# The cosine's argument in turns: one VectorE operation for two in a fused DeltaNet and cosine-gated layer

## The chip, the cores and the metric

The kernel runs on one NeuronCore of a Trainium2 chip. The metric is the device time of one execution in microseconds (us), from the first to the last instruction, as the median of several executions. The core has a matrix engine (TensorE, PE in the profile, with its weight loads listed apart as PEld), a vector engine (VectorE, DVE), an activation engine (ScalarE, ACT), a general engine (GpSimd, POOL) and a queue engine that here only starts transfers (SyncE, SP). Every engine runs its own list of instructions in order and waits on semaphores for the others.

## The reference

Two blocks follow each other. The first is a delta-rule recurrence over 768 steps for 4 batches and 8 heads of width 48. The second multiplies the resulting 3072 x 384 matrix by `w_in` (384 x 2048), applies a gate h cos(h) to each element, and multiplies by `w_out` (2048 x 384).

```python
for t in range(S):
    kt, vt, bt = (k_n[:, :, t], v[:, :, t], beta[:, :, t, None])
    y[:, :, t] = np.einsum('bhd,bhde->bhe', q[:, :, t], state)
    v_old = np.einsum('bhde,bhd->bhe', state, kt)
    state = state + bt[:, :, :, None] * np.einsum('bhd,bhe->bhde', kt, vt - v_old)
...
h = x @ w_in
g = h * np.cos(h)
return (g @ w_out).astype(np.float32)
```

The change lies in the cosine of the second block.

## The kernel before

The recurrence is cut into 24 units of 32 steps. For a pair of units a triangular system is inverted, on VectorE for the first pair and on GpSimd for the other eleven, and carried through DRAM into the shape that the next matmuls want. Each unit then runs through the matmuls `turn`, `gram`, `state`, `solve`, `update`, `within` and `features` on TensorE. A pair of units gives 256 tokens, and these go through the second block as pair p: 8 steps of `hidden`, then the products with `w_out`. For all pairs but the first, those products use Strassen's scheme: seven half-size products for eight, with sums of the gates formed on VectorE (`left_sum`, L829) and the results gathered there (`collect`, L861).

The weights arrive as 64-bit numbers in 28 tiles and are cut down to float32 on the core: a transfer (`narrow_load`), two ScalarE operations (`narrow_split`), two VectorE operations (`narrow_shift`, L414 and L419) and one GpSimd operation (`narrow_add`, L423). The weights are scaled by 256 on the way, so that the first layer's result in PSUM is 256 h (`SCALE = 256.0`).

One step of the first layer computes 2 x 128 hidden features for 256 tokens. It fills a PSUM tile `p_h`, of which there are two; a tile comes free only when the gate has read it. This is the part that the change touches:

```python
def hidden_turns(p, f):                                # ScalarE, L735
    turns[p, f] = ffn_pool.tile([128, 2, TOK], I32, name="turns")
    nc.scalar.activation(
        turns[p, f], p_hs[p, f], AF.Copy, scale=1.0 / (2.0 * math.pi * SCALE)
    )

def hidden_rest(p, f):                                 # VectorE, L742 and L745
    r = rests[p, f] = ffn_pool.tile([128, 2, TOK], FP, name="r")
    n = turns.pop((p, f))
    nc.vector.scalar_tensor_tensor(
        out=r, in0=n, scalar=-PI2_HI * SCALE, in1=p_hs[p, f], op0=ALU.mult, op1=ALU.add
    )
    nc.vector.scalar_tensor_tensor(
        out=r, in0=n, scalar=-PI2_LO * SCALE, in1=r, op0=ALU.mult, op1=ALU.add
    )

def hidden_cos(p, f):                                  # ScalarE, L751 and L752
    r = rests[p, f]
    nc.scalar.activation(r, r, AF.Abs)
    nc.scalar.activation(r, r, AF.Sin, bias=halfpi, scale=-1.0 / SCALE)

def hidden_gate(p, f):                                 # VectorE, L759
    ...
    nc.vector.tensor_tensor(
        out=gates[p, f // 4][:, f % 4 : f % 4 + 2],
        in0=rests.pop((p, f)), in1=p_hs.pop((p, f)), op=ALU.mult,
    )
```

The first operation writes the number of whole turns in h as an integer. The two VectorE operations subtract that many times 2 pi, in two parts of 2 pi so as to keep precision; what is left is an angle between -pi and pi (times 256). The cosine is then the sine of pi/2 minus its absolute value.

The order of the instructions on each engine is fixed when the kernel is written out, by a list scheduler inside the kernel (`class Order`). It knows for each task an engine, a cost in us, what it depends on, and a due time; due times run backward from the `hidden` and output tasks. At each moment an engine takes, of the tasks that may run, the one that is due first, with two rules that matter here: no task may run whose due time is more than `WINDOW` beyond the most urgent one's, and TensorE prefers to stay with small matmuls or with large ones as long as the next of the same sort is due at most `STICK` later:

```python
WINDOW = 82.51
STICK = 2.55
SMALL = ("gram", "state", "solve", "update", "within")
...
W_IN, W_OUT, LOADS = 57.87, 95.11, -8.12      # when weight tiles are due, and their loads
START = 35.79                                 # when the first hidden step is due
FIRST, STEP = 3.55, 5.99                      # pace of the hidden steps, first pair and later ones
BASE = [START + (8 * FIRST + (p - 1) * 8 * STEP if p else 0) for p in range(NU // 2 + 2)]
...
add(("hidden", *key), "PE", 2.62, lambda f=f: hidden(p, f), deps,
    makes=[("h", ("h", *key))], uses=[("x", p)],
    due=BASE[p] + f // 2 * (STEP if p else FIRST))
add(("turns", *key), "ACT", 0.65, lambda f=f: hidden_turns(p, f), ...)
add(("rest", *key), "DVE", 1.45, lambda f=f: hidden_rest(p, f), ...)
add(("cos", *key), "ACT", 1.45, lambda f=f: hidden_cos(p, f), [("rest", *key)])
add(("gate", *key), "DVE", 0.73, lambda f=f: hidden_gate(p, f), ...)
```

The weight tiles arrive in a shared ring of 9 buffers (`GATES = 9`), which the gates use too; a tile holds its buffer until `narrow_add` has read it.

Of the kernel before, what the change touches and what calls it, by code (L numbers as in the profile page):

```python
# [14 lines left out]
ALU = mybir.AluOpType  # L15
AF = mybir.ActivationFunctionType
# [1 line left out]
C = 32  # L18
DP = 64
SPLIT = 2  # L20


PI2_HI = 6.28125
PI2_LO = 2.0 * math.pi - PI2_HI


SCALE = 256.0
# [23 lines left out]
class Order:  # L51
# [6 lines left out]

    WINDOW = 82.51
    LAG = {"PE": 0.2, "DVE": 0.15, "ACT": 0.15, "POOL": 0.2, "SP": 2.0}
    IN_FLIGHT = 8
    STICK = 2.55
    CHANGE = 0.15
    SMALL = ("gram", "state", "solve", "update", "within")

# [12 lines left out]
    def add(  # L80
        self, key, engine, cost, emit, deps=(), makes=(), uses=(), moves=0.0, due=1e9
    ):

        assert key not in self.tasks, key
        self.tasks[key] = [engine, cost, due, emit, set(deps), makes, uses, moves]
        for t in uses:
            self.users[t] = self.users.get(t, 0) + 1
        for tag, t in makes:
            self.tiles[t] = tag
# [19 lines left out]
    def run(self, wrote):  # L109
# [28 lines left out]
        while events:  # L138
# [21 lines left out]
            def fits(key):  # L160
                return all(live[tag] < self.bufs[tag] for tag, _ in self.tasks[key][5])

            dues = list(running.values())
            for heap in ready.values():
                dues.append(min((x[0] for x in heap if fits(x[2])), default=1e9))
            limit = min(dues) + self.WINDOW
            for engine, heap in ready.items():
# [6 lines left out]
                if engine == "PE":  # L174
                    if (item[2][0] in self.SMALL) != small:
                        item = min(
                            (
                                x for x in able
                                if x[0] <= item[0] + self.STICK
                                and (x[2][0] in self.SMALL) == small  # L180
# [43 lines left out]
def kernel(  # L224
# [32 lines left out]
    nc = tc.nc  # L257
# [90 lines left out]
    for b in range(B):  # L348
        nc.gpsimd.dma_start(
            out=bq[C * b : C * b + H].rearrange("p n t -> p (n t)"), in_=beta[b]  # L350
# [6 lines left out]
    halfpi = const.tile([128, 1], FP, name="halfpi")  # L357
# [359 lines left out]
    gates, p_hs, turns, rests, p_os, outs = ({} for _ in range(6))  # L717

    def hidden(p, f):
        p_h = p_hs[p, f] = bank("h", [128, 2, TOK], "p_h")  # L720
        for i in range(2):
            for t in range(KT):
                nc.tensor.matmul(  # L723
                    p_h[:, i],
                    w_in[:, t, (f + i) * 128 : (f + i + 1) * 128],
                    xts[p][:, t],
                    start=(t == 0),
                    stop=(t == KT - 1),
                )

    def hidden_turns(p, f):
        turns[p, f] = ffn_pool.tile([128, 2, TOK], I32, name="turns")
        nc.scalar.activation(  # L735
            turns[p, f], p_hs[p, f], AF.Copy, scale=1.0 / (2.0 * math.pi * SCALE)
        )

    def hidden_rest(p, f):
        r = rests[p, f] = ffn_pool.tile([128, 2, TOK], FP, name="r")  # L740
        n = turns.pop((p, f))
        nc.vector.scalar_tensor_tensor(  # L742
            out=r, in0=n, scalar=-PI2_HI * SCALE, in1=p_hs[p, f], op0=ALU.mult, op1=ALU.add
        )
        nc.vector.scalar_tensor_tensor(  # L745
            out=r, in0=n, scalar=-PI2_LO * SCALE, in1=r, op0=ALU.mult, op1=ALU.add
        )

    def hidden_cos(p, f):
        r = rests[p, f]  # L750
        nc.scalar.activation(r, r, AF.Abs)  # L751
        nc.scalar.activation(r, r, AF.Sin, bias=halfpi, scale=-1.0 / SCALE)  # L752

    def hidden_gate(p, f):
        if f % 4 == 0:
            gates[p, f // 4] = ffn_pool.tile(
                [128, 4, TOK], FP, name="g_ffn", tag="g", bufs=GATES
            )
        nc.vector.tensor_tensor(  # L759
            out=gates[p, f // 4][:, f % 4 : f % 4 + 2],  # L760
            in0=rests.pop((p, f)),
            in1=p_hs.pop((p, f)),
            op=ALU.mult,
        )
# [120 lines left out]
    )  # L885
    add = order.add
    VECTOR = {0: "one"}
    W_IN, W_OUT, LOADS = 57.87, 95.11, -8.12
    PLAIN = range(1)
    outs_done = [None]  # L890
    START = 35.79
    FIRST, STEP = 3.55, 5.99
    BASE = [START + (8 * FIRST + (p - 1) * 8 * STEP if p else 0) for p in range(NU // 2 + 2)]

    def inverse(m):
# [113 lines left out]
    def gated(p):  # L1009
        for f in range(0, FT, 2):  # L1010
            deps = [("features_out", 2 * p + 1)]
            if p == 0:
                deps += [("add", t) for t in range(KT * (f // 4 + 1))]
            if p or f:
                deps.append(("hidden", p if f else p - 1, f - 2 if f else FT - 2))
            key = (p, f)
            add(("hidden", *key), "PE", 2.62, lambda f=f: hidden(p, f), deps,
                makes=[("h", ("h", *key))], uses=[("x", p)],
                due=BASE[p] + f // 2 * (STEP if p else FIRST))
            add(("turns", *key), "ACT", 0.65, lambda f=f: hidden_turns(p, f),  # L1020
                [("hidden", *key)], makes=[("turns", ("turns", *key))])
            add(("rest", *key), "DVE", 1.45, lambda f=f: hidden_rest(p, f),
                [("turns", *key)], makes=[("r", ("r", *key))], uses=[("turns", *key)])
            add(("cos", *key), "ACT", 1.45, lambda f=f: hidden_cos(p, f), [("rest", *key)])
            add(("gate", *key), "DVE", 0.73, lambda f=f: hidden_gate(p, f),
                [("cos", *key)] + ([("gate", p, f - 2)] if f % 4 else []),
                makes=[] if f % 4 else [("g", ("gates", p, f // 4))],
                uses=[("h", *key), ("r", *key)], due=BASE[p] + f // 2 * STEP + 8)
        if p in PLAIN:
            plain(p)  # L1030
        else:
            strassen(p)
# [7 lines left out]
    def plain(p):  # L1040
        last = outs_done[0]
        for i in range(2):
            for k in range(FT // 4):
                deps = [("gate", p, 4 * k), ("gate", p, 4 * k + 2)]
                if p == 0:
                    deps += [("add", 12 + t) for t in range(4 * k + 4)]
                if last:
                    deps.append(last)
                last = ("out", p, i, k)
                add(last, "PE", 2.62, lambda i=i, k=k: output(p, i, k), deps,  # L1050
                    makes=[] if k else [("o", ("p_o", p, i)), ("o", ("p_o2", p, i))],
                    uses=[("gates", p, k)], due=BASE[p + 1] + (4 * i + k + 0.5) * STEP)
            add(("out_out", p, i), "ACT", 0.52, lambda i=i: output_out(p, i), [last],
                makes=[("o_out", ("o", p, i))], uses=[("p_o", p, i), ("p_o2", p, i)],
                due=BASE[p + 1] + (4 * i + 5) * STEP)
            store_task(p, i, [("out_out", p, i)], BASE[p + 1] + (4 * i + 6) * STEP)
        outs_done[0] = last
# [68 lines left out]
    for p in sorted(PLAIN):  # L1126
        gated(p)
    weight_sums()
    for p in range(len(PLAIN), NU // 2):
        gated(p)  # L1130
# [63 lines left out]
```

## Time and profile before

| | before |
|---|---|
| time, median of 3 executions | 717.2 us (714.33 to 720.22) |
| profiled execution | 712.6 us, mean granted TensorE clock 0.963 |
| hidden steps (12 pairs x 8) | 96 |
| first and last matmul of the first layer | 76.0 us, 679.9 us |
| ScalarE in the first layer (L735, L751, L752) | 57.0 + 60.5 + 69.3 us |
| VectorE for the Strassen sums (L829) | 81.6 us |
| GpSimd in the inversions (L580, L587) | 143.7 + 141.4 us |

The page of a profile gives busy time by engine, then the span in 40 slices of 17.8 us each with a digit for the busy tenths, then the chain of waits that ended last, then groups of instructions by source line. A group's row reads: line, engine, operation, what it writes `<-` what it reads, shape and type, how many times; then the total busy time and the mean duration in nanoseconds; then the idle time of the engine just before these instructions, and what ended most of it. Two further views are used: the waits (who waited for whom, in a chosen stretch of time) and a table of busy time by stretch, whose columns are length, then busy time and instruction count of PE, PEld, DVE, ACT and POOL, then the granted TensorE clock, the share of the transfer engines in use and the bytes moved.

### The profile page before, as it was taken

Reading aid. Unit: us, or ns where it says so; the run is one execution under the profiler, and the core shown is the slowest. Engines: PE = TensorE matmul, PEld = TensorE weight load, DVE = VectorE, ACT = ScalarE, POOL = GpSimd, SP = SyncE. Lnnn points to the kernel's source line nnn. Section 1 sums busy time; section 2 is a strip of 40 time slices with the busy share of each in tenths; the row PEclk is TensorE's granted clock in tenths of the full one; section 3 lists DMA queues with packets and bytes.
Section 4 is the critical chain, followed back from the end, with each engine's and each line's share of the span. In section 5 each row is a group of like instructions: output and inputs, shape, how many; then the busy total and the mean of one; then the engine's idle time right before and its main releaser. Section 6 shows DMA issues by size and latency. Waiting matters only on the chain.

```text
span 712.6 us, 25186 instructions
## 1 busy us (share of the span) xinstructions
PE 640.6 (90%) x11000; PEld 562.2 (79%) x11000; DVE 473.9 (66%) x900; ACT 283.1 (40%) x482; POOL 360.3 (51%) x738
## 2 busy tenths in 40 slices
PE   3206988999999999999999999999999999999985
PEld 2205777768888988988988988978988888989985
DVE  4995799996666666666666657656666665665641
ACT  4424376652452452542452442442442532532420
POOL 6368869948608718508718628408618318300000
PEclk9655799999999999999999999999999999999999
DMA  9885692472242152142152141242131210100000
GB/s 175 215 184 138 122 228 63 100 139 53 41 80 48 17 98 55 33 82 55 28 95 47 32 97 40 34 93 42 20 64 41 38 51 14 30 14 13 1 23 22
DMA packets 162701, 49.26 MB, mean 69 GB/s; under 512 B 154208, under 2 KB 157296, under 8 KB 162592
## 3 DMA queue, kind: packets, MB, share of 16 engines
q1 hardware_dynamic: 161120, 46.82, 31.9%
q8 instruction: 86, 1.41, 0.8%
q0 software_dynamic: 384, 0.64, 0.4%
q10 hardware_dynamic: 1088, 0.20, 0.1%
q14 instruction: 23, 0.19, 0.1%
HBM read 36.62 MB, written 11.01 MB: 67 GB/s over the span
## 4 chain that ended last, share of the span: by engine, by line
PE 75%; POOL 6%; DMA 6%; DVE 5%; issue 4%; SPq 2%; ACT 1%; ACTq 0%; DVEq 0%; POOLq 0%
PE p_h L723 31%; PE p_out L813 28%; PE p_kq L622 4%; POOL part L580 3%; POOL z L587 3%; PE p_kq L687 2%; PE p_u L649 2%; PE p_s L670 2%; PE p_g L511 2%; DMA pairs<-in_moe_w_in_dram 2%; PE p_t L493 2%; DMA gb<-g_dr 1%; DMA qp<-in_q_dram 1%; SPq L327 1%; DMA kp<-in_k_dram 1%
## 5 line engine op out<-in xcount | busy, mean ns | idle before, releaser
L723 PE MATMUL p_h<-x_ffn,w_in 128*128 128x256 f32 x1152 | 266.9, 383 | 6.8 <-DVE g_ffn L759 6.8
L723 PEld LDWEIGHTS p_h<-x_ffn,w_in 128*128 128x128 f32 x1152 | 216.0, 191 | 36.8 <-issue 7.1
L580 POOL TENSOR_TENSOR part<-z,gb 128x126 f32<-128x126 f32 (+22 forms) x341 | 143.7, 421 | 106.0 <-DMA gb<-g_dr 63.0
L587 POOL TENSOR_TENSOR z<-z,part 128x126 f32<-128x126 f32 (+22 forms) x341 | 141.4, 415 | 26.7
L813 PE MATMUL p_out<-w_out,g_ffn 128*128 128x192 f32 x704 | 130.5, 333 | 2.7 <-DVE o L861 1.6
L813 PEld LDWEIGHTS p_out<-w_out,g_ffn 128*128 128x128 f32 x704 | 113.2, 190 | 7.9 <-DVE o L861 2.5
L742 DVE SCALAR_TENSOR_TENSOR r<-turns,p_h 128x512 f32<-128x512 int32 x96 | 65.7, 685 | 74.1 <-ACT turns L735 74.0
L735 ACT ACTIVATE turns<-p_h 128x512 int32<-128x512 f32 x96 | 57.0, 593 | 123.1 <-PE p_h L723 123.0
L751 ACT ACTIVATE r<-r 128x512 f32<-128x512 f32 x96 | 60.5, 630 | 109.6 <-DVE r L745 108.2
L759 DVE TENSOR_TENSOR g_ffn<-r,p_h 128x512 f32<-128x512 f32 x96 | 65.7, 684 | 50.7 <-ACT r L752 50.3
L813 PE MATMUL p_out<-w_sum,g_ffn 128*128 128x192 f32 x528 | 97.1, 330 | 2.3 <-DVE o L861 2.3
L813 PEld LDWEIGHTS p_out<-w_sum,g_ffn 128*128 128x128 f32 x528 | 86.6, 190 | 6.7 <-DVE o L861 4.4
L452 POOL TENSOR_TENSOR knrm<-ksum,halves 128x16 f32<-128x16 f32 (+1 forms) x14 | 36.3, 2593 | 107.8 <-DVE ksum L440 103.8
L829 DVE TENSOR_TENSOR g_ffn<-g_ffn 128x256 f32<-128x256 f32 x176 | 81.6, 492 | 8.9 <-PE p_out L813 7.5
L745 DVE SCALAR_TENSOR_TENSOR r<-turns,r 128x512 f32<-128x512 int32 x96 | 71.3, 742 | 3.3
L752 ACT ACTIVATE r<-r,halfpi 128x512 f32<-128x512 f32 x96 | 69.3, 722 | 3.1
L861 DVE SCALAR_TENSOR_TENSOR o<-p_out,o 128x192 f32<-128x192 f32 x77 | 26.3, 354 | 51.9 <-PE p_out L813 46.4
L493 PE MATMUL p_t<-consts,kp 128*128 128x128 f32 x96 | 16.9, 305 | 42.0 <-DVE tt L531 31.8
L493 PEld LDWEIGHTS p_t<-consts,kp 128*128 128x128 f32 x96 | 13.0, 156 | 44.3 <-issue 38.1
L622 PEld LDWEIGHTS p_kq<-st,kq_t 48*32 48x32 f32 x2944 | 29.5, 106 | 6.8 <-issue 6.4
L622 PE MATMUL p_kq<-st,kq_t 48*32 48x48 f32 x2944 | 33.1, 215 | 1.1 <-issue 1.1
L499 ACT COPY kq_t<-p_t 128x512 f32<-128x512 f32 x48 | 25.7, 588 | 10.5 <-PE p_t L493 10.5
(66 smaller groups left out, 559.8 us busy)
## 6 DMA issues: line engine op xcount, KB each, us to landing
pairs<-in_moe_w_in_dram SPq DMA_DIRECT2D x12, 512.0 KB
gb<-g_dr SPq DMA_DIRECT2D x24, 256.0 KB
pairs<-in_moe_w_out_dram SPq DMA_DIRECT2D x16, 384.0 KB
vp<-in_v_dram SPq DMA_DIRECT2D x96, 48.0 KB
out_dram<-o SPq DMA_DIRECT2D x24, 192.0 KB
kp<-in_k_dram SPq DMA_DIRECT2D x92, 48.0 KB
qp<-in_q_dram SPq DMA_DIRECT2D x92, 48.0 KB
g_dr<-g SPq DMA_DIRECT2D x24, 128.0 KB
```

The lines of the kernel that those rows point to most:

```text
L580: eng.tensor_tensor(out=part, in0=z[:, 0:rows, j, None].to_broadcast(shape), in1=a[:, j, None, j + 1 :].to_broadcast(shape), op=ALU.mult,)
L587: eng.tensor_tensor(out=behind, in0=behind, in1=part, op=ALU.subtract)
L622: nc.tensor.matmul(p_kq[quarter(b), par, a, j], kq_t[rows48(par), a, j, quarter(b)], st[rows48(par), b // 2, j, b % 2], start=(j == 0 and ...
L723: nc.tensor.matmul(p_h[:, i], w_in[:, t, (f + i) * 128 : (f + i + 1) * 128], xts[p][:, t], start=(t == 0), stop=(t == KT - 1),)
L735: nc.scalar.activation(turns[p, f], p_hs[p, f], AF.Copy, scale=1.0 / (2.0 * math.pi * SCALE))
L742: nc.vector.scalar_tensor_tensor(out=r, in0=n, scalar=-PI2_HI * SCALE, in1=p_hs[p, f], op0=ALU.mult, op1=ALU.add)
L745: nc.vector.scalar_tensor_tensor(out=r, in0=n, scalar=-PI2_LO * SCALE, in1=r, op0=ALU.mult, op1=ALU.add)
L751: nc.scalar.activation(r, r, AF.Abs)
L752: nc.scalar.activation(r, r, AF.Sin, bias=halfpi, scale=-1.0 / SCALE)
L759: nc.vector.tensor_tensor(out=gates[p, f // 4][:, f % 4 : f % 4 + 2], in0=rests.pop((p, f)), in1=p_hs.pop((p, f)), op=ALU.mult,)
L813: nc.tensor.matmul(p_o, left(p, e // 2, a)[:, e % 2], right(e, b), start=(e == 0), stop=(e == FT // 2 - 1), skip_group_check=True,)
L829: nc.vector.tensor_tensor(out=left(p, k, to), in0=left(p, k, one), in1=left(p, k, two), op=op)
```

## The change

The angle is kept in turns. ScalarE writes the whole number of turns as before, and one VectorE operation computes 256 h / (2 pi 256) minus that number: a fraction of a turn between -1/2 and 1/2. The factor 2 pi moves into the scale of the sine. With no product of a large integer and 2 pi, the second part of 2 pi is not needed. The aim is to halve the VectorE work between the two ScalarE operations of a hidden step.

The scheduler is told the new cost of the step (0.73 us for 1.45), and eight of its constants are new. Whatever the scheduler decides changes with them: the order of tasks on all five engines.

```diff
-    WINDOW = 82.51
+    WINDOW = 133.06
...
-    STICK = 2.55
+    STICK = 4.14
...
+    TURN = 1.0 / (2.0 * math.pi * SCALE)
...
     def hidden_rest(p, f):
         r = rests[p, f] = ffn_pool.tile([128, 2, TOK], FP, name="r")
-        n = turns.pop((p, f))
         nc.vector.scalar_tensor_tensor(
-            out=r, in0=n, scalar=-PI2_HI * SCALE, in1=p_hs[p, f], op0=ALU.mult, op1=ALU.add
-        )
-        nc.vector.scalar_tensor_tensor(
-            out=r, in0=n, scalar=-PI2_LO * SCALE, in1=r, op0=ALU.mult, op1=ALU.add
+            out=r, in0=p_hs[p, f], scalar=TURN, in1=turns.pop((p, f)),
+            op0=ALU.mult, op1=ALU.subtract,
         )
...
-        nc.scalar.activation(r, r, AF.Sin, bias=halfpi, scale=-1.0 / SCALE)
+        nc.scalar.activation(r, r, AF.Sin, bias=halfpi, scale=-2.0 * math.pi)
...
-    W_IN, W_OUT, LOADS = 57.87, 95.11, -8.12
+    W_IN, W_OUT, LOADS = 62.2, 48.42, -16.83
...
-    START = 35.79
-    FIRST, STEP = 3.55, 5.99
+    START = 64.59
+    FIRST, STEP = 4.18, 5.64
...
-            add(("rest", *key), "DVE", 1.45, lambda f=f: hidden_rest(p, f),
+            add(("rest", *key), "DVE", 0.73, lambda f=f: hidden_rest(p, f),
```

More of the change, by code (lines that the diff above doesn't have):

```diff
@@ L20 @@
 SPLIT = 2
-PI2_HI = 6.28125
-PI2_LO = 2.0 * math.pi - PI2_HI
 SCALE = 256.0
@@ L729, in hidden @@
                 )
+    TURN = 1.0 / (2.0 * math.pi * SCALE)
     def hidden_turns(p, f):
         turns[p, f] = ffn_pool.tile([128, 2, TOK], I32, name="turns")
-        nc.scalar.activation(
-            turns[p, f], p_hs[p, f], AF.Copy, scale=1.0 / (2.0 * math.pi * SCALE)
-        )
+        nc.scalar.activation(turns[p, f], p_hs[p, f], AF.Copy, scale=TURN)
     def hidden_rest(p, f):
         r = rests[p, f] = ffn_pool.tile([128, 2, TOK], FP, name="r")
-        n = turns.pop((p, f))
         nc.vector.scalar_tensor_tensor(
-            out=r, in0=n, scalar=-PI2_HI * SCALE, in1=p_hs[p, f], op0=ALU.mult, op1=ALU.add
-        )
-        nc.vector.scalar_tensor_tensor(
-            out=r, in0=n, scalar=-PI2_LO * SCALE, in1=r, op0=ALU.mult, op1=ALU.add
+            out=r, in0=p_hs[p, f], scalar=TURN, in1=turns.pop((p, f)),
+            op0=ALU.mult, op1=ALU.subtract,
         )
```

## The prediction, made before the changed kernel ran

> **What bounds the kernel now.** I read the page from the top: busy time by engine, then the span in slices.
>
> ```profile
> span 712.6 us, 25186 instructions
> PE 640.6 (90%) x11000; PEld 562.2 (79%) x11000; DVE 473.9 (66%) x900; ACT 283.1 (40%) x482; POOL 360.3 (51%) x738
> ...
> PE   3206988999999999999999999999999999999985
> PEld 2205777768888988988988988978988888989985
> DVE  4995799996666666666666657656666665665641
> ...
> PEclk9655799999999999999999999999999999999999
> ```
>
> TensorE is the busiest engine, and from the eighth slice on its row is all nines. VectorE has nines only in slices 2 and 3 and 6 to 9; later it is at six tenths. So the engine that the change relieves bounds at most a piece near the start. To see how much idle TensorE time there is anywhere, I cut the span at the first and last hidden step (76 and 680 us) and at two visible borders, and asked for the busy time in each stretch (length; PE, PEld, DVE, ACT, POOL; clock, transfers).
>
> ```profile
> 0.00:54.00 54.00, 12.02 (x290) 10.17 (x291) 41.09 (x123) 19.59 (x35) 30.44 (x51) 0.73 0.90 190
> 54.00:76.00 22.00, 15.46 (x591) 13.02 (x589) 12.85 (x18) 8.58 (x16) 19.44 (x36) 0.58 0.53 130
> 76.00:150.00 74.00, 67.06 (x1074) 53.21 (x1073) 66.48 (x107) 47.27 (x87) 57.38 (x86) 0.98 0.59 132
> 150.00:680.00 530.00, 523.11 (x8923) 465.20 (x8922) 343.94 (x629) 205.37 (x342) 253.02 (x566) 1.00 0.25 48
> 680.00:712.60 32.60, 22.96 (x130) 20.57 (x128) 9.54 (x25) 2.28 (x4) 0.00 (x0) 0.97 0.08 24
> ```
>
> Length minus PE gives the idle time of TensorE: 42.0, 6.5, 6.9, 6.9 and 9.6 us, together 72 us. The change removes no matmul, so it can only take from these 72 us, from the cost of switching between kinds of matmul (below), or from time at a low clock. The long stretch is 98.7% busy (523.11 of 530). In the third stretch TensorE and VectorE are both at 90% (67.06 and 66.48 of 74).
>
> Which wait ends last there? The waits of TensorE alone, 76 to 150 us:
>
> ```profile
> PE p_h L723 <- DVE g_ffn L759: 5.1, 4, 2.1
> PE p_t L493 <- DVE tt L531: 0.9, 1, 0.9
> ```
>
> Four times a hidden step waits for VectorE's gate to release one of the two `p_h` tiles, 5.1 us in all: the loop matmul, turns, rest, absolute value, sine, gate is longer than the matmuls it hides behind. In 0 to 76 us the same view has a single wait of 29.7 us (`p_t` for `tt`) beside ones of at most 6.9: with the first inverse not back from DRAM there is little else to multiply.
>
> The rows of the step itself:
>
> ```profile
> L742 DVE SCALAR_TENSOR_TENSOR r<-turns,p_h 128x512 f32<-128x512 int32 x96 | 65.7, 685 | 74.1 <-ACT turns L735 74.0
> L735 ACT ACTIVATE turns<-p_h 128x512 int32<-128x512 f32 x96 | 57.0, 593 | 123.1 <-PE p_h L723 123.0
> L751 ACT ACTIVATE r<-r 128x512 f32<-128x512 f32 x96 | 60.5, 630 | 109.6 <-DVE r L745 108.2
> L759 DVE TENSOR_TENSOR g_ffn<-r,p_h 128x512 f32<-128x512 f32 x96 | 65.7, 684 | 50.7 <-ACT r L752 50.3
> L745 DVE SCALAR_TENSOR_TENSOR r<-turns,r 128x512 f32<-128x512 int32 x96 | 71.3, 742 | 3.3
> ```
>
> L745, the operation that goes, is the dearest of the step (742 ns) and releases ScalarE 77 times by the waits view. ScalarE's waiting costs nothing by itself: it is 40% busy.
>
> [...]
>
> **The change, part by part.**
>
> *The operation.* The new one reads `p_h` from PSUM and the integers from SBUF, as L742 does with the order turned, so I take 685 ns. L742 and L745 together are 137.0 us; 96 x 685 ns is 65.8. VectorE loses 71 us, 10% of the span in busy time. Nearly all of it is off the path: 58 us of L745 lie between 150 and 680 us, where TensorE waits for a gate only 1.6 us.
>
> *The latency.* In a quiet step near 663 us, turns begins at 663.46 and the gate ends at 667.64, 4.18 us; without the second operation (0.72 us from start to start) that is 3.46 us. Where VectorE is full it is more, since an operation queued behind others also leaves.
>
> *Stretch 76 to 150.* Fifteen L745 go, 13.0 us of VectorE's 66.5. That more than covers the 6.0 us that TensorE waited for VectorE there. But TensorE is 90% busy and cannot fall below 67 us of work, and other waits move up (weights, the inverse of the second pair). I book 4 us of the 6.9.
>
> *Stretch 150 to 680.* Of 6.9 us idle, the gate accounts for 1.6 and fetching of instructions ("issue") for 3.6. I book 1 us.
>
> *Tail.* After the last hidden step at 680 the last gate comes 0.7 us sooner; the products that follow alternate with their collection (0.45 us each time), which is unchanged. I book 0.7.
>
> *The scheduler's constants.* They move no work, only order. Two things are on the path. First, switches on TensorE: in the chain of waits a group of eight products takes 1.30 us between large neighbours and 1.50 between small ones:
>
> ```profile
> 199.31 1.30 PE p_out L813 x8
> ...
> 205.14 1.50 PE p_out L813 x8
> ```
>
> So a change of kind costs about 0.1 us. Counting along TensorE's timeline I find 169 changes, some 17 us. `STICK` from 2.55 to 4.14 should remove some; I assume 20, hence 2 us. Second, the start. Hidden steps are due 29 us later than before (`START`), weights for the second layer 47 us earlier (`W_OUT`) and loads 9 us earlier. So weight work gains priority over the recurrence. Before, GpSimd ran the second pair's inversion without a break from 39 to 71 us and then eight additions in a row, 10.46 us, while loads waited for ring buffers (transfers at 0.53 in 54 to 76). Interleaving would even that out, but delays the inverse that units 2 and 3 need. I book 0, with 5 us either way.
>
> The sum is 4 + 1 + 0.7 + 2 + 0 = about 8 us: 717.2 - 8 = 709.
>
> **The rivals.** *Hidden anyway:* with TensorE at 98.7% through three quarters of the span, the removed 71 us are idle VectorE time and nothing else, and what is gained near the start is waited for elsewhere; 715 to 718. For it: the chain of waits is 75% TensorE and 5% VectorE. Against: the 5.1 us of gate waits are real and directly behind the removed operation. *The new order is worse:* weight work ahead of the recurrence delays the first inverse or the first hidden step beyond 76 us, with TensorE idle at half clock; each microsecond there is one of the span. 718 to 726. For it: VectorE is full from 18 to 54 us, transfers are at 0.90 up to 54. Against: the constants were presumably chosen for the new cost. *The new order is the larger gain:* the start holds 48.5 of the 72 idle us, so a first hidden step at 66 to 70 with fewer switches later gives 698 to 703. For it: solve to first hidden step takes 20 us now, with weight work of VectorE in between. Against: before 55 us the path is transfers, the inversion on VectorE and the way through DRAM, and no constant shortens those.
>
> **Range and chances.** All gains at their best (6 + 3 + 1 + 4 + 5 = 19 us) give 698; no gain and a start 5 us later give 722. Within these, 697 to 721 should hold 8 in 10. Faster by over 2% means under 702.9 us; that needs the start to improve as well, 0.19. Slower by over 2% means over 731.5, more than any single delay I can find: 0.06. The rest is 0.75.
>
> **What will show it.** The new operation near 685 ns with a maximum under 700; VectorE's busy time near 403 us; the gate waits of TensorE before 150 us under 2 us; TensorE's busy time within a few us of 640 less what the switches give; the changes of kind under 169; the first hidden matmul between 71 and 81 us. I am wrong if the first hidden step moves by more than 5 us, if the long stretch opens gaps (above 12 us idle), or if the new operation, by its operand order, costs clearly more than 685.

## The result, and the profile after

The changed kernel takes 710.8 us against 718.0 for the kernel before (a fourth execution has moved its median from 717.2): ratio 0.9899, 95% interval 0.9855 to 0.9944. Measured again on another occasion it took 712.3 against 717.4, ratio 0.9924 (0.9897 to 0.9951). It is faster by 5 to 7 us, about 1%, as forecast (709, range 697 to 721).

The page of the changed kernel, the lines that answer to those shown of before:

```profile
span 707.4 us, 25090 instructions
...
PE 642.0 (91%) x11000; PEld 564.3 (80%) x11000; DVE 400.3 (57%) x804; ACT 281.5 (40%) x482; POOL 344.1 (49%) x738
...
PE   3206989999999999999999999999999999999985
...
DVE  4995568967655645546546546545635535544441
```

VectorE has lost 73.6 us of busy time (473.9 to 400.3), its row has fallen mostly to fours to sixes after the first quarter, and the span is 5.2 us shorter. TensorE is as busy as it was (640.6, now 642.0). In the table of busy time by stretch, cut at the same times as before (length; PE, PEld, DVE, ACT, POOL; clock, transfers):

```profile
0.00:54.00 54.00, 11.94 (x291) 9.90 (x292) 40.23 (x123) 19.41 (x34) 30.72 (x52) 0.68 0.90 183
54.00:76.00 22.00, 15.51 (x524) 12.99 (x523) 12.58 (x22) 7.90 (x15) 19.57 (x36) 0.50 0.81 178
76.00:150.00 74.00, 69.28 (x1147) 55.72 (x1146) 55.55 (x98) 48.92 (x91) 58.44 (x87) 0.97 0.55 132
150.00:680.00 530.00, 526.74 (x8940) 469.21 (x8939) 284.73 (x543) 204.92 (x342) 235.41 (x565) 1.00 0.24 47
680.00:707.40 27.40, 18.51 (x104) 16.45 (x103) 7.22 (x21) 0.33 (x1) 0.00 (x0) 0.97 0.07 22
```

Idle TensorE time, length minus PE, is now 42.1, 6.5, 4.7 and 3.3 us in the first four stretches; before it was 42.0, 6.5, 6.9 and 6.9. So the gain is in the middle, and the start as a whole is as idle as it was. The last stretch is cut in another place of the work; from the start of the last first-layer matmul to the end it is 32.7 us in both (674.7 to 707.4, and 679.9 to 712.6). The first hidden step starts at 79.2 us for 76.0.

The waits of TensorE alone between 76 and 150 us, and then the rows of the hidden step (busy, mean ns; idle before, and whose doing):

```profile
PE p_kq L618 <- issue: 3.0, 1, 3.0
PE p_h L719 <- DVE g_ffn L751: 1.6, 2, 1.3
```

```profile
L736 DVE SCALAR_TENSOR_TENSOR r<-p_h,turns 128x512 f32<-128x512 f32 x96 | 66.1, 689 | 113.8 <-ACT turns L732 113.7
L732 ACT ACTIVATE turns<-p_h 128x512 int32<-128x512 f32 x96 | 56.9, 592 | 169.1 <-PE p_h L719 169.0
L751 DVE TENSOR_TENSOR g_ffn<-r,p_h 128x512 f32<-128x512 f32 x96 | 65.6, 683 | 48.0 <-ACT r L744 48.0
L743 ACT ACTIVATE r<-r 128x512 f32<-128x512 f32 x96 | 60.7, 632 | 58.2 <-DVE r L736 58.1
```

The new operation costs 689 ns. The gate's waits fell from 5.1 to 1.6 us. In their place stands one wait of 3.0 us under "issue", which means that the profile names nothing that TensorE waited for. In the trace, a transfer of the queue that the page calls "instruction" ends 1.5 us before this wait does (99.63 and 101.10 us), so fetching of instructions is the likely cause.

### The profile page after: what moved, and what is told of

Its sections match the earlier page's. It is cut to its first block, busy times and chain, and to the rows that moved or that the text cites. A ratio compares the mean times of both kernels' runs of the same rounds, so it can differ in the third digit from the quotient of the medians.

```text
span 707.4 us, 25090 instructions
## 1 busy us (share of the span) xinstructions
PE 642.0 (91%) x11000; PEld 564.3 (80%) x11000; DVE 400.3 (57%) x804; ACT 281.5 (40%) x482; POOL 344.1 (49%) x738
## 4 chain that ended last, share of the span: by engine, by line
PE 85%; DMA 4%; POOL 3%; DVE 3%; issue 2%; ACT 1%; SPq 1%; ACTq 0%; DVEq 0%; POOLq 0%
PE p_h L719 35%; PE p_out L805 30%; PE p_kq L618 4%; PE p_kq L683 3%; PE p_s L666 3%; PE p_out L761 3%; PE p_u L645 3%; PE p_t L489 2%; PE p_g L507 2%; DMA pairs<-in_moe_w_in_dram 2%; POOL part L576 1%; POOL z L583 1%; DMA qp<-in_q_dram 1%; DMA gb<-g_dr 1%; DMA kp<-in_k_dram 1%
## 5 line engine op out<-in xcount | busy, mean ns | idle before, releaser
L576 POOL TENSOR_TENSOR part<-z,gb 128x126 f32<-128x126 f32 (+22 forms) x341 | 136.1, 399 | 210.7 <-DMA gb<-g_dr 185.3
L583 POOL TENSOR_TENSOR z<-z,part 128x126 f32<-128x126 f32 (+22 forms) x341 | 134.3, 394 | 26.7
L805 PE MATMUL p_out<-w_out,g_ffn 128*128 128x192 f32 x704 | 133.6, 334 | 2.8 <-DVE o L853 1.6
L736 DVE SCALAR_TENSOR_TENSOR r<-p_h,turns 128x512 f32<-128x512 f32 x96 | 66.1, 689 | 113.8 <-ACT turns L732 113.7
L694 ACT COPY y<-p_kq 128x384 f32<-128x384 f32 x24 | 11.5, 478 | 76.7 <-PE p_kq L683 76.7
L653 DVE TENSOR_TENSOR u<-p_u,bz 128x768 f32<-128x768 f32 x24 | 23.0, 956 | 17.1 <-PE p_u L645 17.1
```

Of the source, the lines that this page charges most:

```text
L576: eng.tensor_tensor(out=part, in0=z[:, 0:rows, j, None].to_broadcast(shape), in1=a[:, j, None, j + 1 :].to_broadcast(shape), op=ALU.mult,)
L583: eng.tensor_tensor(out=behind, in0=behind, in1=part, op=ALU.subtract)
L736: nc.vector.scalar_tensor_tensor(out=r, in0=p_hs[p, f], scalar=TURN, in1=turns.pop((p, f)), op0=ALU.mult, op1=ALU.subtract,)
L805: nc.tensor.matmul(p_o, left(p, e // 2, a)[:, e % 2], right(e, b), start=(e == 0), stop=(e == FT // 2 - 1), skip_group_check=True,)
```

## The experiments

The question was which part did it: the operation, or the order that the scheduler makes of the new constants. The order depends on costs and constants alone, not on what a task emits. So the operation and the order can be exchanged one at a time: the lists of TensorE, ScalarE, GpSimd and SyncE in the first two kernels below are those of the kernel before and of the changed kernel, item by item. Times are medians; each ratio is to the kernel before on the same occasion.

**One operation, old order** (label op_only).

```diff
 # the kernel before; constants and the cost of 1.45 told to the scheduler stay
         nc.vector.scalar_tensor_tensor(
-            out=r, in0=n, scalar=-PI2_HI * SCALE, in1=p_hs[p, f], op0=ALU.mult, op1=ALU.add
-        )
-        nc.vector.scalar_tensor_tensor(
-            out=r, in0=n, scalar=-PI2_LO * SCALE, in1=r, op0=ALU.mult, op1=ALU.add
+            out=r, in0=p_hs[p, f], scalar=1.0 / (2.0 * math.pi * SCALE), in1=turns.pop((p, f)),
+            op0=ALU.mult, op1=ALU.subtract,
         )
...
-        nc.scalar.activation(r, r, AF.Sin, bias=halfpi, scale=-1.0 / SCALE)
+        nc.scalar.activation(r, r, AF.Sin, bias=halfpi, scale=-2.0 * math.pi)
```

> The one-operation angle in the order of the kernel before: the scheduler is still told 1.45 us and keeps its old constants, so all engines but VectorE run the very same list, and VectorE only loses L745 96 times. My theory (the removed operation shortens the gate loop near the start, the constants give the rest): the gate waits of TensorE between 76 and 150 us fall from 5.1 to under 2 us, and the time falls by 4 to 6 us, to 712 to 714 (ratio 0.992 to 0.995). Rival A (VectorE's relief is hidden anyway and the new order is the whole gain): 717 to 718, ratio above 0.997. Rival B (the operation gives all, the new order nothing or a loss): 711 or less, ratio 0.990 or less.

It took 713.6 us against 716.9: ratio 0.9948 (0.9928 to 0.9968), a gain of 3.3 us. That is within the range of my theory, but the waits of TensorE between 77 and 150 us, which were to bring it, did not fall in its profile:

```profile
PE p_h L723 <- DVE g_ffn L756: 5.2, 2, 2.6
```

What holds the gate is seen at 122 us. On ScalarE's timeline the sine of that step starts at 115.02 and takes 0.72 us. The gate (L756) comes 5 us later. This is VectorE's timeline (start, duration) in between, and it has no gap:

```profile
116.32 1.77 DVE L481 TENSOR_TENSOR vp<-vp,knrm 128x768 f32<-128x768 f32 x1
118.01 1.36 DVE L839 TENSOR_TENSOR w_sum<-w_out 128x384 f32<-128x384 f32 x1
119.29 1.35 DVE L414 SCALAR_TENSOR_TENSOR pairs<-pairs 128x384 uint32<-128x384 uint32 x1
120.57 0.58 DVE L419 TENSOR_SCALAR w_out<-w_out 128x384 uint32<-128x384 uint32 x1
121.07 0.67 DVE L756 TENSOR_TENSOR g_ffn<-r,p_h 128x512 f32<-128x512 f32 x1
```

The gate stands in the list behind weight work and recurrence work. My theory had the right engine and the wrong reason: the loop's length was not what made this gate late. The profiled execution is one of the slower ones of this kernel (716.4 us, median 713.6), so its sum of waits is no exact measure; the last section shows what may have slowed it. Rivals A (nothing) and B (everything) fall too.

**Two operations, new order** (order_only).

```diff
 # the kernel before, with the eight new constants and the cost of 0.73;
 # hidden_rest and the sine's scale stay
-    WINDOW = 82.51
+    WINDOW = 133.06      # and STICK, W_IN, W_OUT, LOADS, START, FIRST, STEP
...
-            add(("rest", *key), "DVE", 1.45, ...
+            add(("rest", *key), "DVE", 0.73, ...
```

> The order of the changed kernel with the two old operations: the cost told to the scheduler and the eight constants are new, so all engines but VectorE run the changed kernel's list. My theory: the order alone is worth about 2 us, 715 to 717 (ratio 0.996 to 0.999), since the gate waits near the start come back. Rival A (order is everything): 710 to 711, ratio 0.990. Rival B: 718 to 721, ratio 1.000 to 1.004, because the first hidden step starts 3 us later in this order and nothing pays for it.

It took 725.4 us, ratio 1.0104 (1.0077 to 1.0131). The new order with the old operations is slower than anything I had allowed for. Together with the second measurement of the changed kernel, made on another occasion (717.4 us for the kernel before), the four corners are:

| | old order | new order |
|---|---|---|
| two operations | 716.9 | 725.4 |
| one operation | 713.6 | 712.3 |

The operation is worth 3.3 us in the old order and 13.1 in the new one; the order costs 8.5 us with two operations. With one it gains 1.3 us by these medians, which is within the noise: the ratios 0.9948 (0.9928 to 0.9968) and 0.9924 (0.9897 to 0.9951) overlap. So the gain can't be divided into a share of the operation and a share of the order: the new order is only as good as the old one because the step is shorter. From its first to its last hidden step the waits of TensorE are led by:

```profile
PE p_h L723 <- DVE g_ffn L759: 7.5, 11, 3.1
PE p_kq L622 <- issue: 3.4, 3, 2.1
```

Eleven gate waits here, two in the changed kernel with the same list.

**One operation, true cost, old constants** (op_cost).

```diff
 # one operation; the eight constants of the kernel before
-            add(("rest", *key), "DVE", 1.45, ...
+            add(("rest", *key), "DVE", 0.73, ...
```

> One operation, the scheduler told 0.73 us, but the eight constants of the kernel before. If the constants carry a gain of their own beyond the operation, this stays 1 to 3 us above the changed kernel (712 to 714, ratio 0.992 to 0.994). If telling the true cost is what matters, it equals the changed kernel (710 to 711, ratio 0.990). If the old constants fit only the old cost, it is worse than the one operation in the old order.

It took 719.6 us, ratio 1.0034 (1.0016 to 1.0053): 6 us slower than the same operation with the untrue cost. Telling the scheduler the truth, with constants chosen for another cost, throws the gain away. The third expectation held.

**One operation, true cost, only WINDOW and STICK new** (only_ws).

```diff
 # op_cost, and of the constants
-    WINDOW = 82.51
+    WINDOW = 133.06
-    STICK = 2.55
+    STICK = 4.14
```

> One operation, cost 0.73, and of the constants only the two of the scheduler's rules, WINDOW 133.06 and STICK 4.14; the due times stay old. TensorE's list has 148 changes between small and large matmuls instead of 168. By my price of about 0.1 us for a change it should be 2 us under the same kernel with the old two rules (op_cost). If the price is not real in the total, no difference; if larger groups make the recurrence wait longer, it is slower by 1 to 3 us.

It took 729.1 us, ratio 1.0153 (1.0128 to 1.0179). Its 148 changes of kind instead of 166 do not save it, and none of the three expectations held: it is 9 us slower than op_cost, where the first hidden step starts at 76.9 us; here it starts at 87.6. From first to last hidden step it needs 605.7 us against 608.2 of op_cost, so the 2 us for fewer changes may be real, but here they come with nearly 11 us lost at the start.

**One operation, true cost, only the due times new** (no_ws).

```diff
 # op_cost, and of the constants
-    W_IN, W_OUT, LOADS = 57.87, 95.11, -8.12
+    W_IN, W_OUT, LOADS = 62.2, 48.42, -16.83
-    START = 35.79
-    FIRST, STEP = 3.55, 5.99
+    START = 64.59
+    FIRST, STEP = 4.18, 5.64
```

> One operation, cost 0.73, new due times (START, FIRST, STEP, W_IN, W_OUT, LOADS) with the old WINDOW and STICK. With all old constants it was 719.6, with only WINDOW and STICK new 729.1, with all new 711 to 712. If the due times carry the gain, 711 to 714. If the two groups work only together, 717 or more.

It took 743.1 us, ratio 1.0346 (1.0316 to 1.0376). The two groups work only together. TensorE's timeline shows the cost at the start (start, duration, operation, and in brackets the idle time before and its cause):

```profile
60.33 1.94 PE L649 MATMUL p_u<-vp,zt 32*32 32x48 f32 x64 [33.84 <-DMA zt<-z_dr]
75.91 1.55 PE L670 MATMUL p_s<-u,kp 64*64 64x96 f32 x32 [13.65 <-DVE tt L531]
95.12 8.39 PE L723 MATMUL p_h<-x_ffn,w_in 128*128 128x256 f32 x24 [0.66 <-ACT x_ffn L712]
```

The recurrence's first `p_s` waits 13.65 us for a `tt` on VectorE, and the first hidden step starts at 95 us. From 63.2 to 74.3 us VectorE's timeline has sixteen weight operations (L414 and L419) without a gap, and this `tt` only at 75.35. Weight work has gone ahead of the recurrence, the second rival of the prediction, here in full.

**The changed kernel again** (after_again), unchanged, as a yardstick.

> The changed kernel itself, as a yardstick on the chip of this set: 710 to 711, ratio 0.990, as first measured.

712.3 us, ratio 0.9924, as told above: 1 us more than expected.

**A third operation in the old order** (three_ops).

```diff
+        nc.vector.scalar_tensor_tensor(
+            out=r, in0=n, scalar=0.0, in1=r, op0=ALU.mult, op1=ALU.add
+        )
```

> The kernel before, in its own order, with a third VectorE operation of the kind of L745 in each hidden step (it adds zero times the integers to the angle, so the result is unchanged). Theory now: an order has slack for the VectorE work it was chosen with; in the old order one operation fewer gave 3.3 us, while in the new order one more cost 14.6. If that asymmetry is a property of adding against removing, a third operation in the old order costs 8 us or more (725 to 735). Rival: the effect of one operation is linear in the old order and large only in the new one: then it costs 3 to 4 us (720 to 721).

It took 734.4 us, ratio 1.0252 (1.0220 to 1.0284). One operation less gives 3.3 us, one more costs 17: these orders have room for the work that they were made for and little beyond. This agrees with the 13 us of the second operation in the new order. The first line of the waits of TensorE between 74.7 and 150 us:

```profile
PE p_h L723 <- DVE g_ffn L762: 9.3, 4, 4.1
```

Four waits, 9.3 us, where the kernel before has 5.1; after 150 us there are nine more with 5.5 us in all. By 150 us it has done 156 matmuls of the first layer (1152 less the 996 after), the kernel before 180 (1152 less 972).

**START half a microsecond earlier, in the changed kernel and in the kernel before** (jit_after, jit_before).

```diff
-    START = 64.59
+    START = 64.09        # jit_after
-    START = 35.79
+    START = 35.29        # jit_before
```

> The changed kernel with START at 64.09 for 64.59: a change of meaning so small that no due time matters by itself, but the scheduler's ties fall differently and all engines get another list. If the constants carry understanding (where work is put), it stays at 710 to 712. If they are a draw from a spread of orders, out of which one was picked, it falls back toward the other orders with one operation that were measured: 714 to 722.

> The kernel before with START at 35.29 for 35.79, otherwise unchanged, two operations. If the old constants are a picked draw as well, it is slower than the kernel before by 2 to 8 us (719 to 725); if half a microsecond of a due time means nothing, it is 716 to 718.

Both shifts reorder the lists, and neither matters beyond the noise: 712.4 us, ratio 0.9938 (0.9911 to 0.9966), beside 0.9924 (0.9897 to 0.9951) for the changed kernel, and 717.5 us, ratio 1.0001 (0.9986 to 1.0016). In the second, TensorE waits 7.5 us for gates up to 150 us, for 5.1 in the kernel before, and the time is the same. The suspicion that each set of constants is one lucky draw among neighbours is not borne out for this constant and this step; a new cost in op_cost did move the time by 6 us.

**VectorE's weight operations shortened, with two operations and with one, old order** (light_before, light_op). Both leave out the narrowing of most of each weight tile on VectorE, so the weights are not the reference's and only the times are of use.

```diff
-            out=lo, in0=hi, scalar=0x80000000, in1=lo,
+            out=lo[:, 0:16], in0=hi[:, 0:16], scalar=0x80000000, in1=lo[:, 0:16],
...
-        nc.vector.tensor_scalar(w, w, 3, None, op0=ALU.logical_shift_left)
+        nc.vector.tensor_scalar(w[:, 0:16], w[:, 0:16], 3, None, op0=ALU.logical_shift_left)
```

> The kernel before with VectorE's two weight operations (L414, L419) cut to 16 columns of each tile, so that most weights stay unfinished and the output is not the reference's; the instructions, their order and their waits stay, only their length goes. Theory now: near the start the gate is late because weight operations stand ahead of it in VectorE's list, and not because the loop of the hidden step is long. Then the gate waits between 76 and 150 us fall from 5.1 to under 2.5 us with both old operations in place, and the time falls by 3 to 6 us (711 to 714). Rival (the loop's own length, or the transfers of the weights, makes the gate late): waits stay above 4 us and the time within 2 us of the kernel before.

> The same shortened weight operations with one operation in the hidden step, old order. If weight operations in VectorE's list are what keeps the gate late, they were also what kept the removed operation from showing: gate waits before 150 us under 2 us (5.2 with full weight operations) and 3 to 5 us off the 713.6 of the one operation in the old order, 709 to 711. If the gate hangs on the weights' transfers and ScalarE's part of them, the waits at about 96 and 122 us stay and so does the time, 712 to 714.

711.8 us, ratio 0.9915 (0.9885 to 0.9946), and 708.5 us, ratio 0.9865 (0.9832 to 0.9897). The gate's line in the waits of TensorE from the first hidden step to 150 us, light_before and then light_op:

```profile
PE p_h L723 <- DVE g_ffn L759: 1.8, 2, 1.0
```

```profile
PE p_h L723 <- DVE g_ffn L756: 0.9, 1, 0.9
```

So it is weight work on VectorE that keeps the gate late near the start: with it short, the waits fall from 5.1 to 1.8 us although both old operations are there, and the time by about 6 us. At 122 us the list of op_only shows directly that the gate stands behind this work; shorter weight operations may also free the weights' buffers sooner, and these runs do not separate the two. One half of the expectation fell: the shorter weight work does not make the removed operation worth more. It is worth 3.4 us here (711.8 to 708.5) and 3.3 us with full weight operations. By these medians the two add up, but by the intervals the two differences are uncertain by 1.5 to 3 us.

**A PSUM tile of its own for every second product of the last pair** (tail), on the changed kernel.

```diff
+    def apart(p, x):
+        return p == NU // 2 - 1 and list(PRODUCTS).index(x) % 2 == 1
+
+    def place(p, x):
+        if not apart(p, x):
+            return p_out[:, (p + list(PRODUCTS).index(x)) % 2, 0:HM]
+        if (p, x) not in places:
+            places[p, x] = bank("one", [128, 256], "p_far")[:, 0:HM]
+        return places[p, x]
...
-        p_o = p_out[:, (p + list(PRODUCTS).index(x)) % 2, 0:HM]
+        p_o = place(p, x)
...
-                    makes=[] if part else [("o", ("p_o", p, x))],
+                    makes=[] if part else [("one" if apart(p, x) else "o", ("p_o", p, x))],
```

> The changed kernel with every second product of the last pair in a PSUM tile of its own instead of the other half of the shared one; the order differs only in the last 30 us. In the tail each product waits 0.45 us until the one before is collected, though it writes the other half. If the shared tile is the cause, six such waits go, 2 to 3 us: 708 to 710, below both kernels. If the waits come from the sums that VectorE forms between products, nothing changes: 711 to 712.

It took 706.9 us, ratio 0.9841 (0.9813 to 0.9869), faster than both kernels and than expected. In the changed kernel a product waits for the collection of the one before, though it writes the other half of the tile; two such products on TensorE's timeline of the changed kernel, then two of this one:

```profile
686.40 2.87 PE L805 MATMUL p_out<-w_sum,g_ffn 128*128 128x192 f32 x16 [0.51 <-DVE o L853]
689.72 2.87 PE L805 MATMUL p_out<-w_sum,g_ffn 128*128 128x192 f32 x16 [0.45 <-DVE o L853]
```

```profile
684.66 2.76 PE L817 MATMUL p_out<-w_sum,g_ffn 128*128 128x192 f32 x16
687.26 2.76 PE L817 MATMUL p_far<-w_sum,g_ffn 128*128 128x192 f32 x16
```

Start to start falls from 3.32 to 2.60 us, without a wait, and from the last first-layer matmul to the end it is 28.3 us for 32.7. So the shared tile is the cause. Whether the memory itself or the dependencies set for a tile as a whole make TensorE wait, the run doesn't show.

## Why the prediction was right, point by point

*The bound.* TensorE with 72 us idle was the right account: it has 65.4 idle now (707.4 less 642.0), and 71 us less VectorE work was forecast where 73.6 came off, for a gain of 5 to 7 us in time.

*The operation's cost*: 685 ns forecast, 689 measured, with a maximum of 694. Holds.

*Stretch 76 to 150, 4 us.* In the changed kernel the gate waits are 1.6 us, under the 2 forecast; the idle time fell only by 2.2 us (6.9 to 4.7), since "issue" waits grew there from 0.3 to 3.0 us. But the reason failed. I had the removed operation shorten the loop until TensorE no longer waits; in the old order the operation went and the profile still has 5.2 us of gate waits. What op_only's list and the light kernels show in its place is weight work ahead of the gate. The chain of waits of the kernel before had it already: from 112.5 to 117.8 us it runs through VectorE's L414, L419, L481, L842, L414 and L419, and then the gate.

*Stretch 150 to 680, 1 us.* Mis-sized. Idle time fell by 3.6 us (6.9 to 3.3): the gate waits went from 1.6 us to none, "issue" waits from 3.6 to 1.3. The two stretches together gave 5.8 us for the 5 booked, and the gate waits in them fell by 5.1 us (6.7 to 1.6); the "issue" waits only lie elsewhere (3.9 us before, 4.3 now). In the old order, too, the gate's waits after 150 us fall to 0.3 us without the second operation (from 1.6, in op_only and in light_op alike). They do so as well in jit_before with both operations, so where the 3.3 us of the old order lie stays open.

*Tail, 0.7 us.* Did not come: 32.7 us before and after. The last sine ends at 677.90 us, but the gate starts only at 679.60: in VectorE's list it stands behind two collections that wait for TensorE's products. Counted from the last first-layer matmul, it starts 4.9 us later for 5.2 before.

*Fewer changes of kind, 2 us.* Failed outright: counted in the same way there are 168 in both kernels. I had taken `STICK` by itself, out of eight constants that act together. With `WINDOW` and `STICK` alone there are 148 changes (only_ws), and that kernel is slower.

*The start, 0 with 5 us either way.* The first hidden step is 3.2 us later and the idle time up to it equal (48.5 us of 76.0 before, 48.6 of 79.2 now). TensorE has done more of the recurrence by then, 951 instructions for 879.

So the sum came out near because the two middle stretches gave 5.8 us for 5 booked; the two terms that failed (2 and 0.7) made it too high, about 8 us against 5.2 between the profiled executions and 5 to 7 in the medians. That it holds is in part luck: the prediction treated the parts as if they added. The table of four corners shows that they don't: as single changes they are worth 3.3 us and minus 8.5, together 5.1. The rival "new order is worse" is what the order is without the operation; "hidden anyway" holds for all but 3 of the 71 us in the old order.

What stays open is why these constants fit one operation and cost 8.5 us with two: the runs show where the waits are, not which of the eight makes them, as the two groups alone give 729.1 and 743.1.

## What to carry to other kernels

In a kernel with a fixed order, a shorter operation off the critical path may give little by itself (here 3.3 us of 71); its worth depends on the order around it (13.1 us in the new one), so measure operation and order apart and together. Look at what stands ahead of the late instruction in its own engine's list before blaming the chain it belongs to. And look at the end of the span, where nothing overlaps any more: the shared tile, which cost the changed kernel 0.4 us of waits up to the last hidden step, cost 4 us there.

## What the runs showed of the hardware

Some waits of TensorE cost up to twice what they show, since the matmuls after them took longer (in op_only at 121.89 us, 2.56 us of wait and then 2.63 us more than in the kernel before). In op_only twelve matmuls took 4.51 us after a wait of 2.60 us and 5.46 us after one of 2.56 us, for 2.83 after a wait of 2.08 us in the kernel before; TensorE's timeline of op_only, then of the kernel before:

```profile
96.18 4.51 PE L723 MATMUL p_h<-x_ffn,w_in 128*128 128x256 f32 x12 [2.60 <-DVE g_ffn L756]
121.89 5.46 PE L723 MATMUL p_h<-x_ffn,w_in 128*128 128x256 f32 x12 [2.56 <-DVE g_ffn L756]
```

```profile
94.97 2.83 PE L723 MATMUL p_h<-x_ffn,w_in 128*128 128x256 f32 x12 [2.08 <-DVE g_ffn L759]
```

During the group of the kernel before the granted clock is 1.00. In the changed kernel twelve matmuls took 4.53 us, from 101.33 us on, after the wait of 2.99 us under "issue", and the granted clock during them is 0.62. In op_only it is 0.91 from 77 to 150 us, for 0.98 in the kernel before from 76 to 150. The length of the wait alone does not decide: after a wait of 2.03 us in order_only twelve matmuls took 4.51 us, after one of 2.08 us in the kernel before 2.83.

Against 2.83 us for twelve matmuls, the longer groups after such waits add up to an excess of 4.3 us in op_only's profile, 6.0 in order_only, 5.4 in three_ops and 1.7 in the changed kernel (after its 3.0 us of "issue"); the kernel before has none. That is enough to explain why the profiled execution of op_only lies 2.8 us above its median. And a part of what a little more VectorE work costs (12 us in order_only and 20 in three_ops, between profiled executions) is this and not the wait itself.

GpSimd's busy time follows the operation and not the order: 360.3 and 361.2 us with two operations (before, order_only), 343.4 and 344.1 with one (op_only, after), 374.1 with three, although GpSimd's list in op_only is that of the kernel before. The operations taken away or added read two SBUF tiles. In the kernel before L745 takes 691 to 1492 ns, and all 29 of its 96 that exceed 700 ns run while GpSimd is busy; of the other 67, 50 do not. L742 and the new operation, which read one tile from PSUM, never exceed 693 and 694 ns, though 47 and 54 of their 96 run while GpSimd is busy. And in that trace the 58 GpSimd operations of the inversion (L580, L587) after 150 us that overlap an L745 take on average 205 ns more than the median of their line and shape without it, 11.9 us in all; the 88 that overlap an L742 take 25 ns less. So both engines take longer where these two run at once; by what mechanism, no run shows. What the shorter GpSimd work is worth stays open: TensorE's waits name none on GpSimd, before or after, but the chain of waits of the kernel before runs through the inversion on GpSimd for some 30 us from 153.5 us on, and in the changed kernel the chain has no GpSimd work from 148 to 190 us.
